# Windowed attention and token/channel mixer on one core: the first batch's units in one written list, and other groups of u with an identity matmul

## The chip, the cores and the metric

The kernel runs on one core of one Trainium2 chip. The metric is the device time of one execution in microseconds (us). The engines are called as in the profile: PE (TensorE matmuls), PEld (its weight loads), DVE (VectorE), ACT (ScalarE), POOL (GpSimd), SP (SyncE).

## The reference, cut to what matters

Four batches, 8 heads, 768 rows, head size 64. Each row attends to the 128 rows that end with itself and to the first four rows (the sinks). The heads' results side by side are x (768 x 512 for a batch), which goes through two mixers:

```python
scores = scale * np.matmul(q, k.transpose(0, 1, 3, 2))
keep = is_sink | in_window
a = np.exp(scores - max) ; a = a / np.sum(a)          # over the kept keys
x = np.matmul(a, v)                                   # heads side by side
h = np.maximum(x.T @ w_tok1, 0.0) @ w_tok2            # along the 768 rows
u = x + h.T
out = u + np.maximum(u @ w_ch1, 0.0) @ w_ch2          # along the 512 columns
```

## The kernel before, in words

Heads go in pairs, four pairs to a batch (p = 0 to 3 in the first). q and k of the first batch's pairs are loaded by SP and cast on chip by ACT, DVE or POOL (POOL for pair 3); all later ones come by casting loads that POOL issues. The work on PE is cut into **units**. A unit names its PE cost, what it depends on, how many banks of PSUM it needs, and the operations on other engines that follow it (`then`). There are two banks' worth of `sc` (scores, two physical banks each) and four `mx` banks. Units of the first batch, by the names that the change gives them (p the pair, g a group):

- **q0, k0, ...**: `turn` (L429) transposes q or k of a pair into two `mx` banks; two copies by ACT or DVE (L402, lines 129 and 131 in the profile) make qT, kT.
- **m00, m01, ...**: `masked` (L484) writes the additive mask of pair p, key group g into a score bank with identity matmuls (`ps_sc<-mask_add,ident`). All but m30 exist; s30 is masked afterwards, on DVE (L547).
- **s00, ...**: `scores` (L499) adds the scores into that bank (`ps_sc<-qT,kT`); then ACT takes the exponential (L539, `pT`). g is 0, 1, 2; g = 2 is narrower (768 columns for 1024).
- **x1, x3**: `score_sinks` (L561), the sink scores of two pairs (`ps_mx<-qT,kT`), then an exponential (L578).
- **o00, o01, ...**: `pv` (L586), probabilities times v for half the rows, in one `mx` bank; then DVE takes the reciprocal of the sums (L607) and normalises into x_sb (L610).
- **h00, h01, h10, h11**: `mix_h` (L706), x times w_tok1 for column group g (g = 0 is pairs 0 and 1) and half t of the 256 token features; a relu on ACT or DVE makes h1T.
- **u00, u02, u04, u10, u12, u14**: `mix_u` (L734), h times w_tok2 for group g and two row tiles from st. With `by_pe`, x is added in PSUM by one identity matmul for each row tile, and the result may be copied out by ACT or DVE; without, DVE alone takes it out and adds x (L751).
- **t00, ...**: `transpose_u` (L800) transposes these two row tiles of u (`ps_mx<-ident,u_sb`); a copy makes uT.

Then the channel mixing of batch 0 starts: `v1` (L892, `ps_mx<-uT,w_ch`), which needs both column groups of uT. The attention of the later batches is woven into it.

What orders the work is a planner that runs as the program is built (`Plan.run`, L319). It keeps a clock for each engine, with costs written beside each operation, and writes out, step after step, the unit or operation that can begin first by these clocks. There are three sources of PE units: `main` (channel mixing), `side` (attention and token mixing of later batches, placed behind `main` units as the list MERGED says; k4 and q4, the turned k and q of pair 4, are its first two) and `first` (the first batch). `first` holds several lists, in falling priority. At each step only the heads of the lists are looked at, and the first list whose head can begin within 40 ns of the soonest is taken (95 ns when staying in 64-row matmuls):

```python
early = [(t, u) for u in first if u for t in [self.start_pe(u[0])] if t is not None]
if early:
    soonest = min([t for t, _ in early] + ([] if t is None else [t]))
    stay = [(t, u) for t, u in early if self.half and u[0].half and t <= soonest + SWITCH]
    te, u = next((e for e in stay + early if e[0] <= soonest + (SWITCH if e in stay else 40.0)), (None, None))
```

Operations on ACT, DVE and POOL are taken whenever they can begin first, on the engine that would end them first. On the chip each engine then runs its instructions in the written order. `first_attention` (L822) gives six lists: scores, masks, turns, values (o), the token mixing of group 1, that of group 0. The order that came out on PE, read off the trace:

```
q0 k0 m00 m01 s00 s01 q1 m02 k1 s02 m10 x1 s10 m11 q2 s11 o00 m12 k2 s12 o01 m20 q3 s20 m21 k3 s21 o10 m22 o11
s22 s30 x3 h00 m31 m32 s31 s32 o20 o21 h01 o30 o31 u00 u02 u04 h10 h11 t00 t02 t04 u10 u12 u14 t10 t12 t14
```

With `by_pe` are u00, u02, u04 and u12.

Of the kernel before, what the change touches and what calls it, by code (L numbers as in the profile page):

```python
# [16 lines left out]
def kernel(  # L17
# [16 lines left out]
    NT = S // P  # L34
# [5 lines left out]
    NTOK = DTOK // P  # L40
    NHP = H // 2
# [11 lines left out]
    )  # L53
    NQ = 6
    NPT = 3
# [65 lines left out]
    def mm(*args, **kwargs):  # L121
        in_order(nc.tensor.matmul(*args, skip_group_check=True, **kwargs))  # L122
# [28 lines left out]
    def keep_warm(n, slot):  # L151
# [18 lines left out]
        out=ident, in_=ident, compare_op=ALU.not_equal, fill=1.0, base=0, pattern=[[-1, P]], channel_multiplier=1,  # L170
    ))
    in_order(nc.gpsimd.affine_select(
        out=mask_add[:, :, 0], in_=mask_add[:, :, 0], compare_op=ALU.is_ge,
# [3 lines left out]
        out=mask_add[:, :, 1], in_=mask_add[:, :, 1], compare_op=ALU.is_ge,  # L177
# [16 lines left out]
    for n in range(4):  # L194
# [3 lines left out]
            out=v_sink_f[rows, odd::2, i, 0:D],  # L198
# [167 lines left out]
    def burst(*pieces):  # L366

        need = {}
        for p in pieces:
            for tag, banks in p.need.items():  # L370
                need.setdefault(tag, []).extend(banks)

        def run():
            for p in pieces:
                p.fn()

        op = unit(
            sum(p.size for p in pieces), run, [d for p in pieces for d in p.deps], need,
            [t for p in pieces for t in p.then], half=True,
        )  # L380
        for p in pieces:
            for key in p.keys:
                done[key] = op
        return op
# [44 lines left out]
    def turn(p, n):  # L429

        name = ("q", "k")[n]

        def run():
            ps = [bank("mx", NT, D, dtype=BF16) for _ in range(2)]
            tiles["ps_" + name, p] = [t.rearrange("d j p -> d p j") for t in ps]
            for j in range(NT):
                for x in range(2):
                    rows = ds(D * x, D)
                    in_order(nc.tensor.transpose(ps[x][:, j], bfs[p, n][rows, j], ident[rows, rows]))

        readers = [[op] for op in done[name + "T", p]]
        done["t" + name, p] = unit(
            180, run, [done[name + "_bf", p]], {"mx": readers}, [op for r in readers for op in r], half=True,
        )
        return done["t" + name, p]
# [38 lines left out]
    def masked(p, g):  # L484

        def run():
            ps = tiles["ps_s", p, g] = bank("sc")
            for i in range(2):
                mm(
                    of_keys(ps)[:, i, 0:width(g)], ident,  # L490
                    mask_adds[g == 0].rearrange("p k n q -> p (k n q)")[:, 0:width(g)], start=True, stop=False,
                )

        x = done["exp", p, g] = Op({}, None)
        deps = [done["tk", 0]] if p == 0 else []
        done["mask", p, g] = unit(width(g) * 0.84, run, deps, {"sc": [[x]]})
        return done["mask", p, g]

    def scores(p, g):  # L499

        by_pe = ("mask", p, g) in done
        quarters = p >= NHP and g > 0

        def by_halves(ps):
            for k in range(2):
                kt = 2 * g + k
                nq = 2 if kt < NT - 1 else 1
                for i in range(2):  # L510
                    mm(
                        of_keys(ps)[:, i, ds(2 * k * P, nq * P)], tiles["kT", p][ds(D * i, D), ts(kt, P)],
                        tiles["qT", p][ds(D * i, D), kt * P:(kt + nq) * P], start=not by_pe, stop=True,
                    )

        def by_quarters(ps):
            for k in range(2):
                for y in range(2):
                    a = 4 * g + 2 * k + y
                    nq = min(3, 2 * NT - a)  # L520
                    for i in range(2):
                        rows = ds(D * i, D)
                        mm(
                            ps[ds(D * y, D), i, k, y:y + nq], tiles["kT", p][rows, ts(a, D)],
                            tiles["qT", p][rows, D * a:D * (a + nq)], start=True, stop=True,
                        )

        def run():
            if ("pT", p) not in tiles:
                tiles["pT", p] = pt_pool.tile([P, 2, NT, 2, P], BF16, name="pT")  # L530
            if not by_pe:
                tiles["ps_s", p, g] = bank("sc")
            (by_quarters if quarters else by_halves)(tiles["ps_s", p, g])

        def part(t):
            return t.rearrange("p i k n q -> p i (k n q)")[:, :, 0:width(g)]

        def exp(e):
            in_order(nc.scalar.activation(  # L539
                part(tiles["pT", p][:, :, ds(2 * g, 2)]), of_keys(tiles["ps_s", p, g])[:, :, 0:width(g)], AF.Exp,  # L540
                scale=scale,
            ))

        def mask(e):
            pt = part(tiles["pT", p][:, :, ds(2 * g, 2)])
            m = part(mask_first if g == 0 else mask_main)
            in_order(nc.vector.tensor_tensor(out=pt, in0=pt, in1=m, op=ALU.mult))  # L547

        x = done["exp", p, g] if by_pe else Op({}, None)
        x.cost, x.fn, x.deps = {"ACT": 190.0 + 1.5 * width(g)}, exp, [("pv", p - NPT)] if p >= NPT else []  # L550
        x.urgent = 2 * (p < NHP)
        then = [x]
        if not by_pe:
            then.append(Op({"DVE": 100.0 + 1.2 * width(g)}, mask, [x, done["masks"]]))
            then[-1].urgent = 2 * (p < NHP)
        done["p", p, g] = then[-1]
        deps = [*done["qT", p], *done["kT", p]] if g else [done["qT", p][0], done["kT", p][0]]
        deps += [done["mask", p, g]] if by_pe else []
        return piece((190, 165, 140)[g] if quarters else width(g) * 0.47, run, deps, {} if by_pe else {"sc": [[x]]}, then, [("s", p)])

    def score_sinks(p):  # L561


        def run():
            pT_sink = pt_pool.tile([P, (NT - 2) * P], BF16, name="pT_sink")
            tiles["ps_sk", p] = bank("mx", (NT - 2) * P)
            for n in (p - 1, p):
                tiles["pT_sink", n] = pT_sink
                for i in range(2):
                    rows = ds(D * i, D)  # L570
                    c = ODD * (n % 2)
                    mm(
                        tiles["ps_sk", p][ds(D * i + c, ODD)], tiles["kT", n][rows, 0:ODD],
                        tiles["qT", n][rows, 2 * P:], start=True, stop=True,
                    )

        def exp(e):
            in_order(nc.scalar.activation(tiles["pT_sink", p], tiles["ps_sk", p], AF.Exp, scale=scale))  # L578

        x = Op({"ACT": 580.0}, exp, [("pv", p - NPT)] if p >= NPT else [])  # L580
        for n in (p - 1, p):
            done["p", n, NT] = x
        deps = [d for m in (p - 1, p) for d in [done["kT", m][0], *done["qT", m]]]
        return piece(225, run, deps, {"mx": [[x]]}, [x], [("sk", p - 1), ("sk", p)])
# [236 lines left out]

    def first_attention():  # L822

        for p in range(NHP):
            prepare(p)
        turned = [turn(p, n) for p in range(NHP) for n in range(2)]
        masks, scored, out = [], [], []
        for p in range(NHP):
            for g in range(NT // 2):
                if (p, g) in MASKED_BY_PE:  # L830
                    masks.append(masked(p, g))
                scored.append(burst(scores(p, g)))
                if g == 0 and p == NHP - 1:
                    scored.append(burst(score_sinks(p)))
            if p == 1:
                out.append(burst(score_sinks(p)))
            if p % 2:
                out += [pv(n, half) for n in (p - 1, p) for half in range(2)]
        tokens = []
        for g in range(2):  # L840
            tokens.append([mix_h(0, g, t, 1) for t in range(NTOK)])
            tokens[g] += [mix_u(0, g, st, 2, g == 0 or st == 2) for st in range(0, NT, 2)]
            tokens[g] += [transpose_u(0, g, st, 2) for st in range(0, NT, 2)]
        return scored, masks, turned, out, *tokens[::-1]

    def attention_and_tokens():

# [247 lines left out]
```

## Time and profile before

| what | value |
|---|---|
| median of 3 runs | 207.12 us (206.72 to 207.36) |
| the profiled execution's own time | 206.41 us |
| its span, first to last instruction | 204.6 us |
| granted TensorE clock over the span | 1.000 |
| PE matmuls, busy | 197.6 us |
| the landing of w_tok1 (issued by POOL at 11.39) | 18.9 us |
| first matmul of v1 (channel mixing of batch 0) | 30.46 us |

All other times in the text are of the profiled execution, counted from the start of its span. A row of the timeline is a run of like instructions on one engine: start, length, engine, line, operation, output<-inputs, shape, count, and in brackets how long the engine was idle before it and what released it. Matmuls are pipelined: a row's length has the way through the array in it, so how long a unit holds PE is read from the starts of matmuls, from one unit to the next. `mm` (L121) and `transpose` (L124) record most of PE's work, so units are told apart by their tiles.

### The profile page before, as it was taken

To read this page: it belongs to the slowest core of one execution; us is meant where nothing else is said; L and a number is where in the kernel's file an instruction comes from. 1 tells how busy PE (TensorE), PEld (TensorE's weight loads), DVE (VectorE), ACT (ScalarE), POOL (GpSimd) and SP (SyncE) were. 2 spreads that over 40 slices of the span, in tenths; PEclk is the share of its full clock that TensorE was granted. 3 is DMA by queue.
4 is the path that set the end of the run, shared out by engine and by line. 5 is a ranking of instruction groups with operands and counts; after the bars stand their busy time and mean duration, and the time that the engine had idled before them with its cause. 6 is when DMAs were issued, how large, how long until landed. Compare 5 with 4: busy or idle time off the path is not lost.

```text
span 204.6 us, 5496 instructions
## 1 busy us (share of the span) xinstructions
PE 197.6 (97%) x2377; PEld 119.3 (58%) x2377; DVE 112.4 (55%) x238; ACT 113.8 (56%) x195; POOL 67.3 (33%) x86
## 2 busy tenths in 40 slices
PE   6798999999999999999999999999999999999994
PEld 2345985566665665667656545666655645665453
DVE  4775653657788766866948557572654361001222
ACT  4898668879706535886563145886750114773000
POOL 6299859795699891450000000000000000000000
DMA  6999999999999999193001112100002112000223
GB/s 193 292 257 188 169 177 191 160 172 206 157 180 189 187 184 198 22 128 20 3 0 54 53 64 97 51 5 0 0 3 103 51 54 103 0 3 0 103 103 103
DMA packets 73223, 21.58 MB, mean 105 GB/s; under 512 B 63216, under 2 KB 70256, under 8 KB 73200
## 3 DMA queue, kind: packets, MB, share of 16 engines
q0 software_dynamic: 67232, 11.80, 73.1%
q1 hardware_dynamic: 5968, 9.45, 13.1%
q8 instruction: 18, 0.29, 0.6%
q14 instruction: 5, 0.04, 0.1%
HBM read 26.75 MB, written 6.29 MB: 161 GB/s over the span
## 4 chain that ended last, share of the span: by engine, by line
PE 85%; DMA 6%; DVE 3%; ACT 2%; POOL 1%; issue 1%; SPq 0%; POOLq 0%; ACTq 0%
PE ps_mx L122 77%; PE ps_sc L122 4%; DMA w_tok<-in_moe_w_tok_dram 4%; DMA v_sink_f<-in_v_dram 2%; PE ps_sc L455 2%; POOL v_aug L115 1%; DVE kT L131 1%; PE ps_mx L427 1%; ACT pT L539 1%; ACT qT L129 1%; PE ps_mx L125 1%; SPq L197 0%; ACT uT L129 0%; DVE u_sb L751 0%; DVE x_sb L650 0%
## 5 line engine op out<-in xcount | busy, mean ns | idle before, releaser
L122 PE MATMUL ps_mx<-uT,w_ch 128*128 128x384 bf16 x384 | 67.1, 326 | 0.1
L122 PE MATMUL ps_mx<-w_ch,v1T 128*128 128x512 bf16 (+2 forms) x312 | 66.9, 363 | 0.0
L539 ACT ACTIVATE pT<-ps_sc 128x1024 bf16<-128x1024 f32 (+1 forms) x48 | 44.4, 952 | 13.0 <-PE ps_sc L122 12.9
L122 PEld LDWEIGHTS <-w_ch 128*128 128x128 bf16 x384 | 36.0, 98 | 23.9 <-issue 1.2
L135 ACT ACTIVATE v1T<-ps_mx 128x384 bf16<-128x384 f32 x77 | 37.7, 490 | 19.5 <-PE ps_mx L122 18.9
L122 PEld LDWEIGHTS <-v1T 128*128 128x128 bf16 x312 | 28.3, 98 | 27.6 <-issue 0.5
L924 DVE TENSOR_TENSOR o_sb<-ps_mx,u_sb 128x512 f32<-128x512 f32 x23 | 15.8, 687 | 34.6 <-PE ps_mx L122 34.6
L122 PEld LDWEIGHTS <-w_tok 128*128 128x128 bf16 x192 | 18.3, 98 | 5.9 <-DMA w_tok<-in_moe_w_tok_dram 0.7
L107 POOL DMA_DIRECT2D q_bf<-in_q_dram x24 | 19.6, 822 | 4.4 <-DMA w_ch<-in_moe_w_ch_dram 2.2
L107 POOL DMA_DIRECT2D k_bf<-in_k_dram x24 | 19.6, 820 | 4.1 <-DMA w_ch<-in_moe_w_ch_dram 1.7
L751 DVE TENSOR_TENSOR u_sb<-ps_mx,x_sb 128x512 bf16<-128x512 f32 x20 | 13.2, 687 | 13.0 <-PE ps_mx L122 12.9
L115 POOL DMA_DIRECT2D v_aug<-in_v_dram x16 | 16.4, 1026 | 8.3 <-ACT v_sink L129 7.1
L131 DVE COPY kT<-ps_sc 128x768 bf16<-128x768 bf16 x11 | 10.5, 958 | 13.4 <-ACT qT L129 13.4
L122 PEld LDWEIGHTS <-pT 128*128 128x128 bf16 x352 | 14.1, 98 | 3.3 <-issue 0.6
L129 ACT ACTIVATE qT<-ps_sc 128x768 bf16<-128x768 bf16 x11 | 8.9, 810 | 12.3 <-PE ps_sc L455 12.1
L122 PE MATMUL ps_mx<-v_aug,pT 128*128 128x65 bf16 x352 | 15.6, 194 | 0.0
L547 DVE TENSOR_TENSOR pT<-pT,mask_main 128x1024 bf16<-128x1024 bf16 (+1 forms) x24 | 14.3, 619 | 1.3 <-ACT pT L539 1.3
L122 PE MATMUL ps_sc<-qT,kT 64*64 64x192 bf16 (+3 forms) x288 | 14.4, 248 | 0.0
L135 ACT ACTIVATE h1T<-ps_mx 128x512 bf16<-128x512 f32 (+1 forms) x8 | 4.1, 517 | 17.1 <-PE ps_mx L122 16.9
L122 PE MATMUL ps_mx<-h1T,w_tok 128*128 128x256 bf16 x96 | 13.2, 273 | 0.0
L137 DVE TENSOR_SCALAR v1T<-ps_mx 128x384 bf16<-128x384 f32 x19 | 10.4, 549 | 4.9 <-PE ps_mx L122 4.9
L122 PE MATMUL ps_mx<-x_sb,w_tok 128*128 128x256 bf16 x96 | 12.0, 273 | 0.5 <-DMA w_tok<-in_moe_w_tok_dram 0.4
(68 smaller groups left out, 156.6 us busy)
## 6 DMA issues: line engine op xcount, KB each, us to landing
out_dram<-o_sb SPq DMA_DIRECT2D x23, 256.0 KB, 2.0
v_aug<-in_v_dram POOLq DMA_DIRECT2D x16, 192.0 KB, 7.2
w_ch<-in_moe_w_ch_dram POOLq DMA_DIRECT2D x8, 384.0 KB, 8.8
q_bf<-in_q_dram POOLq DMA_DIRECT2D x24, 96.0 KB, 6.8
k_bf<-in_k_dram POOLq DMA_DIRECT2D x24, 96.0 KB, 5.9
q_f<-in_q_dram SPq DMA_DIRECT2D x4, 384.0 KB, 5.0
k_f<-in_k_dram SPq DMA_DIRECT2D x4, 384.0 KB, 5.7
w_tok<-in_moe_w_tok_dram POOLq DMA_DIRECT2D x2, 384.0 KB, 7.7
```

Source lines behind the costliest of these rows:

```text
L107: in_order(nc.gpsimd.dma_start(out=out[:, h], in_=rows[:, h]))
L115: in_order(nc.gpsimd.dma_start(out=v_aug.rearrange("p i t d -> p (i t) d")[:, :, 0:D], in_=v[b].rearrange("h s d -> (h s) d")[2 * hp * S:2 ...
L122: in_order(nc.tensor.matmul(*args, skip_group_check=True, **kwargs))
L129: in_order(nc.scalar.activation(out, in_, AF.Copy))
L131: in_order({"DVE": nc.vector, "POOL": nc.gpsimd}[e].tensor_copy(out=out, in_=in_))
L135: in_order(nc.scalar.activation(out, in_, AF.Relu))
L137: in_order(nc.vector.tensor_scalar_max(out=out, in0=in_, scalar1=0.0))
L455: in_order(nc.tensor.transpose(ps[:, x, n, j], bfs[p, n][rows, j], ident[rows, rows]))
L539: in_order(nc.scalar.activation(part(tiles["pT", p][:, :, ds(2 * g, 2)]), of_keys(tiles["ps_s", p, g])[:, :, 0:width(g)], AF.Exp, scale=scale,
L547: in_order(nc.vector.tensor_tensor(out=pt, in0=pt, in1=m, op=ALU.mult))
L751: in_order(nc.vector.tensor_tensor(out=u_part(b, g, s0, n), in0=tiles["ps_u", b, g, s0], in1=x_sb[b][:, s0:s0 + n, c0:c0 + cn], op=ALU.add,))
L924: in_order(nc.vector.tensor_tensor(out=o_sb.rearrange("p (g c) -> p g c", g=2), in1=u_rows(b, st), in0=tiles["ps_out", b, st].rearrange("p ...
```

## The change

`first_attention` makes the same units, but gives them a name each and returns one list, in the order of the new constant FIRST_BATCH. So the planner sees one head at a time: the order of these units on PE is the written one. Which engine makes a copy, the place of the operations of ACT and DVE, and the choice of PSUM banks still come from the planner's clocks. `main` and `side` may still go before a head that would begin over 40 ns later.

Against the order of before: s01 before s00; k1 before m02; o01 before m12 k2 s12; s20 before q3; m22 o11 s22 o10 s30 for o10 m22 o11 s22 s30; m31 h01 m32 and h00 after o21, for h00 m31 m32 and h01 after o21; u02 before u00. And x is added by identity matmuls in u02, u12 and u14, where it was u00, u02, u04 and u12.

```diff
+    FIRST_BATCH = (
+        "q0 k0 m00 m01 s01 s00 q1 k1 m02 s02 m10 x1 s10 m11 q2 s11 o00 o01 m12 k2 s12 m20 s20 q3 m21 k3 s21 "
+        "m22 o11 s22 o10 s30 x3 m31 h01 m32 s31 s32 o20 o21 h00 o30 o31 u02 u00 u04 h10 h11 t00 t02 t04 u10 "
+        "u12 u14 t10 t12 t14"
+    )
...
         for p in range(NHP):
             prepare(p)
-        turned = [turn(p, n) for p in range(NHP) for n in range(2)]
-        masks, scored, out = [], [], []
+        made = {}
+        for p in range(NHP):
+            for n in range(2):
+                made["qk"[n] + str(p)] = turn(p, n)
         for p in range(NHP):
             for g in range(NT // 2):
                 if (p, g) in MASKED_BY_PE:
-                    masks.append(masked(p, g))
-                scored.append(burst(scores(p, g)))
-                if g == 0 and p == NHP - 1:
-                    scored.append(burst(score_sinks(p)))
-            if p == 1:
-                out.append(burst(score_sinks(p)))
+                    made[f"m{p}{g}"] = masked(p, g)
+                made[f"s{p}{g}"] = burst(scores(p, g))
             if p % 2:
-                out += [pv(n, half) for n in (p - 1, p) for half in range(2)]
-        tokens = []
+                made[f"x{p}"] = burst(score_sinks(p))
+                for n in (p - 1, p):
+                    for half in range(2):
+                        made[f"o{n}{half}"] = pv(n, half)
         for g in range(2):
-            tokens.append([mix_h(0, g, t, 1) for t in range(NTOK)])
-            tokens[g] += [mix_u(0, g, st, 2, g == 0 or st == 2) for st in range(0, NT, 2)]
-            tokens[g] += [transpose_u(0, g, st, 2) for st in range(0, NT, 2)]
-        return scored, masks, turned, out, *tokens[::-1]
+            for t in range(NTOK):
+                made[f"h{g}{t}"] = mix_h(0, g, t, 1)
+            for st in range(0, NT, 2):
+                made[f"u{g}{st}"] = mix_u(0, g, st, 2, (g, st) in [(0, 2), (1, 2), (1, 4)])
+            for st in range(0, NT, 2):
+                made[f"t{g}{st}"] = transpose_u(0, g, st, 2)
+        return [[made[name] for name in FIRST_BATCH.split()]]
```

## The prediction, made before the changed kernel was run

> **What bounds the kernel now.** I read the page first, then the chain that ended last in order of time, then the timelines of PE, ACT and DVE up to 31 us. The page:
>
> ```profile
> span 204.6 us, 5496 instructions
> PE 197.6 (97%) x2377; PEld 119.3 (58%) x2377; DVE 112.4 (55%) x238; ACT 113.8 (56%) x195; POOL 67.3 (33%) x86
> PE 85%; DMA 6%; DVE 3%; ACT 2%; POOL 1%; issue 1%; SPq 0%; POOLq 0%; ACTq 0%
> ```
>
> PE is busy for 97% of the span, so the end moves by the PE work that goes and by the PE pauses that close. The change touches the first batch alone, and the chain shows where that batch hands over:
>
> ```profile
> 11.39 7.51 DMA w_tok<-in_moe_w_tok_dram
> 18.95 0.83 PE ps_mx L122 x6
> ...
> 27.53 1.54 PE ps_mx L122 x14
> 29.08 0.02 issue
> 29.10 0.70 DVE u_sb L751
> 29.80 0.05 issue
> 29.85 0.40 PE ps_mx L125 x4
> 30.25 0.28 PE ps_mx L439 x12
> 30.53 1.41 PE ps_mx L122 x8
> ```
>
> Up to 18.95 us w_tok1's landing leads; then PE; then a wait for an addition on DVE (u14) before t14; then k4 and the first v1 of the channel mixing (start 30.46 on PE). From there to 201.7 us matmul starts in the trace lie more than 0.2 us further apart than their widths only at 70.56, 72.73 and 98.75, so a shift of the 30.46 goes through to the end. PE before that:
>
> ```profile
> 15.78 0.35 PE L439 MATMUL ps_mx<-ident,k_bf 64*128 64x64 bf16 x12 [0.36 <-POOL k_bf L131]
> 17.62 0.56 PE L122 MATMUL ps_sc<-qT,kT 64*128 64x256 bf16 x8
> 18.95 0.83 PE L122 MATMUL ps_mx<-x_sb,w_tok 128*128 128x256 bf16 x6 [0.45 <-DMA w_tok<-in_moe_w_tok_dram]
> 20.47 0.56 PE L122 MATMUL ps_sc<-qT,kT 64*128 64x256 bf16 x8
> 23.43 0.27 PE L122 MATMUL ps_mx<-x_sb,ident 128*128 128x256 bf16 x1
> ```
>
> and ACT with its exponentials (the second row is s22 and s30, the third s31 and s32):
>
> ```profile
> 16.59 1.02 ACT L539 ACTIVATE pT<-ps_sc 128x1024 bf16<-128x1024 f32 x1
> 18.00 1.73 ACT L539 ACTIVATE pT<-ps_sc 128x768 bf16<-128x768 f32 x2 [0.40 <-PE ps_sc L122]
> 20.90 1.73 ACT L539 ACTIVATE pT<-ps_sc 128x1024 bf16<-128x1024 f32 x2 [0.69 <-PE ps_sc L122]
> ```
>
> To be seen: ACT waits 0.40 us for s22 and 0.69 us for s31, because PE sends o10, m22 and o11 ahead of s22, then stops 0.45 us at h00 for the weights with m31 and m32 queued behind it. The order on PE makes these pauses.
>
> **Prices**, from starts on PE: turn 0.18 us; m 0.43 (narrow g=2: 0.32); s 0.23 (0.15); x 0.21; o 0.38 (first half), 0.55 (second); h 0.65; t 0.22; one identity matmul of u 0.109, so a u is 0.65 with and 0.44 without. Exponentials follow each other on ACT every 0.90 us (0.76 for 768 columns). From a matmul's last column to its reader on ACT or DVE 0.21 us (u12's last matmul starts at 28.35, its reader at 28.66); from an ACT or DVE end to PE 0.05.
>
> **The switch.** Last matmul of m32 starts at 20.210 and streams 0.162, s31 starts at 20.469: 0.10 us for going from 128-row to 64-row matmuls. The list has two more such changes (s22, o10, s30 for s22, s30); they are in the walk below. The Trainium skill, TensorEngine Tiling (Array Packing), section Key Properties, says that a change of tiling mode drains TensorE, which speaks against the new order. The trace agrees, with 0.10 us each; counted fully the two would be 0.2 us of the forecast, and without them it would be 206.3.
>
> **Early part (to 15.78).** s01 goes ahead of s00. s01 needs the second half of kT0 (ACT, to 7.08), s00 only the first, so ACT's first exponential starts at 7.57 (7.13 + 0.12 + 0.11 + 0.21) for 7.33: 0.24 us late. ACT is dense from there to 14.47, so this is carried. k1 ahead of m02 comes 0.3 us earlier (its cast ends at 8.46), o01 ahead of k2 makes kT2 later: k2 at about 13.5 for 12.71, s12's exponential at 14.0 to 14.25 for 13.71. Against this, s20 no longer stands behind q3 (which waits for POOL's cast at 14.26), so its exponential can start by about 15.0 for 15.17. All meets at k3: POOL ends its cast at 15.72, and POOL's order holds no PE result, so k3 stays at 15.78. m22 needs s20's exponential over by 16.24; it is over at 15.9 to 16.05. I take the early part at 0; ends: -0.1 and +0.5.
>
> **Middle part, by start on PE.** s21 15.97; m22 16.30; o11 16.62; s22 17.27, its exponential 17.63 (18.00 before; ACT is done with s21's at 17.49); o10 17.52; s30 18.00; x3 18.33; m31, whose bank s22's exponential leaves at 18.49, 18.64 (19.62 before); h01 19.07, weights there since 18.9; m32, bank free at 19.51, 19.73; s31 20.15, its exponential 20.59 (20.90 before); s32 20.38; o20 20.63 instead of 20.96. **-0.33 us.** The same five units as before follow (2.47 us), so the first u starts at 23.10. Ends: 0 (h01 or m32 wait as long as h00 did) and -0.45 (the whole stop).
>
> **Late part.** Group 0's u lose two pairs of identity matmuls: 4 x 0.109 = -0.44. Group 1 gains one pair: +0.22. **Net -0.22.** u00, u04 and u10 are now added on DVE (0.69 each, where an ACT copy is 0.60). u00 would be read at 24.4 to 25.1 and u04 to 25.8, behind the normalisations of o30 and o31; their transposes come at 25.9 and 26.4, so this is hidden by h10 and h11 (1.31 us); without that cover it would cost up to 0.7. h10 needs o31 normalised by 24.63, and that is over at about 24.3. u10 at 26.61, u12 27.05, u14 27.70, t10 28.35. u10's addition, on DVE after two uT copies as before, is over by 28.0. u12's copy ends on ACT at 28.51: t12 at 28.57 without the 0.19 of before. u14 can now go to ACT: 28.56 to 29.16, t14 29.22, an idle 0.43 in place of 0.30. **-0.08.** What is late next is this copy, on which t14, k4 and v1 stand. Ends: 0.69 on DVE behind two copies, +0.5; or k4 in the idle 0.43, -0.28.
>
> No unit here issues a DMA, and SP's and POOL's queues keep their order. Loads follow each other by landings: k of pair 5 lands at about 24.73 + 7.6 = 32.3, its use is at 33.7, so 0.6 us earlier still fits.
>
> **Sum.** -0.33 - 0.22 - 0.08 = -0.63: v1 starts at 29.83. The profiled execution took 206.41 (its span 204.6 and 1.8 around it), below the runs' 206.72 to 207.36; it would become 205.8. The median 207.12 becomes **206.5**.
>
> **Rivals.**
> 1. *ACT's early delay is not absorbed.* If ACT also takes both halves of kT2 and of kT1 (0.38 each), s20's exponential ends past 16.24 and m22, s22 and all behind them slip by 0.3 to 0.5: 206.8 to 207.0. For it: ACT is dense from 7.3 to 14.5. Against: DVE has pauses there.
> 2. *It does not do what it says.* The order is worked out in the planner's costs, and its landing and copy times are not the chip's: the heads of the one list wait where three lists had another unit. If h01 or m32 pauses as h00 did (-0.33 gone) and t14 waits on DVE (+0.3): 207.1 to 207.2. Against: the walk uses measured rows and finds no pause over 0.1 us between 16 and 28.5.
> 3. *More.* k4 falls into t14's wait, or the stops at 70.56 and 72.73 (0.2 each) close: 205.9 to 206.2. Against: k4 wants two of four banks, which are full of t and u then.
> 4. *Slower, at 70.56.* The planner shares the copies between ACT and DVE by its own clock, which the change shifts. There the chain runs over ACT (pT, uT, qT) and DVE (kT 0.96, reciprocals, x_sb 0.56) and PE already waits 0.2. One more relu (0.55) or uT copy (0.96) put ahead on DVE is a wait of its full length; from 0.63 on the gain is gone, and with both of them, or the same at 98.75, +0.9: 207.4 to 208.0. For it: a full DVE from 68.4 to 70.5. Against: the order of PE from 30.18 on is fixed and its needs are unchanged.
>
> **Numbers.** A difference of 0.3% (0.62 us) is about what a measurement of this kernel can tell from none; the forecast stands on that bound. Forecast (206.2 to 206.8) 0.52, rival 1 0.14, rival 2 0.08, rival 3 0.12, rival 4 0.14. Faster by over 0.3%: rival 3 and somewhat over half of the forecast case, 0.44. Slower by over 0.3%: the greater part of rival 4, 0.12. Within: 0.44. For 8 in 10 the range leaves out the far parts of rivals 3 and 4: 205.9 to 207.5.
>
> **What would show it.** Early: first exponential near 7.6, k3 at 15.78. Middle: s22's exponential near 17.6, m31 before h01 with no long wait, o20 near 20.6. Late: six identity matmuls of x_sb for eight, t12 without a wait, v1 at 29.8. Wrong if k3 or s21 starts later than 16.0, if o20 is not before 20.9, if t00 or t04 waits for DVE, or if PE pauses over 0.3 us stand at 66 to 73 or near 98.

## The result, and the profile after

The changed kernel takes 206.17 us (median of 8 runs, 205.60 to 206.46), the kernel before beside it 206.98 (8 runs, 206.50 to 207.81): ratio 0.9955, interval 0.9937 to 0.9973, about 0.9 us less. Two further comparisons, among the experiments, gave 0.9983 (0.9962 to 1.0003) and 0.9972 (0.9948 to 0.9996). The mean of the three is 0.9970, or 0.62 us of 207. The forecast was 206.5 us, 0.63 us less.

The profiled execution of the changed kernel took 206.46 us, as long as the longest of its 8 runs; that of before, 206.41, was shorter than any of its own. So laid side by side these two show no gain, and the first task is to see why. The page of the changed kernel:

```profile
span 204.7 us, 5470 instructions
PE 197.8 (97%) x2355; PEld 120.0 (59%) x2375; DVE 113.9 (56%) x241; ACT 112.5 (55%) x192; POOL 67.3 (33%) x86
PE 88%; DMA 3%; ACT 3%; DVE 3%; issue 1%; SPq 1%; ACTq 0%
```

The third line is the share of each engine in the chain that ended last: DMA has fallen from 6% to 3%. The chain itself, in order of time (start, length, what), in two stretches:

```profile
2.24 6.41 DMA k_f<-in_k_dram
...
8.67 0.57 DVE k_bf L136
...
15.16 0.71 ACT pT L544
15.87 0.04 issue
15.91 0.59 PE ps_sc L127 x2
16.50 0.28 PE ps_mx L444 x12
...
19.73 0.82 PE ps_mx L127 x6
...
```

```profile
29.23 0.61 ACT u_sb L134
29.83 0.05 issue
29.88 0.40 PE ps_mx L130 x4
...
```

Two things are new. The row at 19.73 is h01, and it now stands behind PE's own work; before, the row at that place, h00, stood behind w_tok1's landing. And the copy ahead of t14 is ACT's (u14, line 134), where it was an addition on DVE. The v1 that closes the batch starts at 30.49 on PE, for 30.46 before: the loads arrived later in this execution. DVE's first cast of q ended at 8.22 instead of 7.48, POOL's chain of work began with the landing of v_sink at 9.61 instead of 8.83, and POOL's cast for k3 ended at 16.34 instead of 15.73. PE from there, on the timeline:

```profile
16.43 0.35 PE L444 MATMUL ps_mx<-ident,k_bf 64*128 64x64 bf16 x12
17.90 0.34 PE L127 MATMUL ps_sc<-qT,kT 64*128 64x256 bf16 x4
18.64 0.39 PE L127 MATMUL ps_sc<-qT,kT 64*128 64x256 bf16 x4
19.29 0.39 PE L127 MATMUL ps_sc<-mask_add,ident 128*128 128x512 bf16 x1
19.73 0.82 PE L127 MATMUL ps_mx<-x_sb,w_tok 128*128 128x256 bf16 x6
23.77 0.27 PE L127 MATMUL ps_mx<-x_sb,ident 128*128 128x256 bf16 x1
29.88 0.40 PE L130 MATMUL ps_mx<-ident,u_sb 128*128 128x128 bf16 x4 [0.24 <-ACT u_sb L134]
```

These are k3, s22, s30, m31, h01, the first u and t14. From k3 to h01 no bracket shows a pause; the one for the weights (0.45 us before) is gone. ACT's exponentials:

```profile
17.20 2.96 ACT L544 ACTIVATE pT<-ps_sc 128x1024 bf16<-128x1024 f32 x3
21.25 1.73 ACT L544 ACTIVATE pT<-ps_sc 128x1024 bf16<-128x1024 f32 x2 [0.27 <-PE ps_sc L127]
```

s21, s22 and s30 follow each other without the 0.40 us of before, and s31 waits 0.27 where it waited 0.69. The start differs between executions, whatever the kernel, so the stages are compared by lengths from k3's start on, all from starts on PE (us, good to 0.01):

| profiled execution | k3 starts | k3 to o20 | o20 to first u | to h10 | to t10 | to t14 | to v1 | k3 to v1 | v1 to last matmul |
|---|---|---|---|---|---|---|---|---|---|
| before | 15.78 | 5.18 | 2.47 | 1.96 | 3.51 | 0.95 | 0.61 | 14.68 | 171.00 |
| before, again | 15.87 | 5.59 | 2.47 | 1.97 | 3.51 | 0.94 | 0.62 | 15.10 | 170.99 |
| changed | 16.43 | 4.87 | 2.47 | 1.53 | 3.73 | 0.85 | 0.61 | 14.06 | 171.00 |
| changed, again | 15.95 | 4.87 | 2.48 | 1.52 | 3.73 | 0.85 | 0.61 | 14.06 | 171.00 |
| changed, third | 16.84 | 4.87 | 2.48 | 1.52 | 3.73 | 0.85 | 0.61 | 14.06 | 171.00 |

From k3 on the changed kernel repeats to 0.01 us; the kernel before does not, and all of its scatter is in one column, k3 to o20. What v1 starts then takes 171.00 us in both.

### The profile page after: what moved, and what is told of

Same layout as the page of the kernel before. It is cut to its first block, busy times and chain, and to the rows that moved or that the text cites. A ratio compares the mean times of both kernels' runs of the same rounds, so it can differ in the third digit from the quotient of the medians.

```text
span 204.7 us, 5470 instructions
## 1 busy us (share of the span) xinstructions
PE 197.8 (97%) x2355; PEld 120.0 (59%) x2375; DVE 113.9 (56%) x241; ACT 112.5 (55%) x192; POOL 67.3 (33%) x86
## 4 chain that ended last, share of the span: by engine, by line
PE 88%; DMA 3%; ACT 3%; DVE 3%; issue 1%; SPq 1%; ACTq 0%
PE ps_mx L127 77%; PE ps_sc L127 6%; DMA k_f<-in_k_dram 3%; PE ps_sc L460 2%; ACT pT L544 1%; PE ps_mx L444 1%; DVE kT L136 1%; PE ps_mx L432 1%; ACT qT L134 1%; SPq L99 1%; DVE x_sb L655 1%; PE ps_mx L130 1%; ACT uT L134 0%; DVE o_sb L933 0%; ACT u_sb L134 0%
## 5 line engine op out<-in xcount | busy, mean ns | idle before, releaser
L127 PE MATMUL ps_mx<-w_ch,v1T 128*128 128x512 bf16 (+2 forms) x295 | 65.1, 362 | 1.1 <-issue 0.3
L933 DVE TENSOR_TENSOR o_sb<-ps_mx,u_sb 128x512 f32<-128x512 f32 x23 | 15.8, 688 | 34.6 <-PE ps_mx L127 34.6
L756 DVE TENSOR_TENSOR u_sb<-ps_mx,x_sb 128x512 bf16<-128x512 f32 x21 | 13.8, 687 | 12.8 <-PE ps_mx L127 12.5
L127 PE MATMUL ps_sc<-qT,kT 64*64 64x192 bf16 (+3 forms) x288 | 15.0, 252 | 0.1
L127 PEld LDWEIGHTS <-kT 64*64 64x64 bf16 (+2 forms) x320 | 7.7, 101 | 8.0 <-issue 4.7
```

Source lines behind the costliest of these rows:

```text
L756: in_order(nc.vector.tensor_tensor(out=u_part(b, g, s0, n), in0=tiles["ps_u", b, g, s0], in1=x_sb[b][:, s0:s0 + n, c0:c0 + cn], op=ALU.add,))
L933: in_order(nc.vector.tensor_tensor(out=o_sb.rearrange("p (g c) -> p g c", g=2), in1=u_rows(b, st), in0=tiles["ps_out", b, st].rearrange("p ...
```

## The experiments

Open after the result were: what in the old order makes k3 to o20 long and variable (the pauses of ACT, as the prediction had it, or w_tok1's landing alone); whether the identity matmuls pay by themselves; and what the early part is worth, since k3 itself starts anywhere from 15.8 to 17.1. The rival theories were that the order of s22 and s31 in front of ACT does it, and that the new early order makes POOL's chain to k3 shorter. The three groups below ran on one chip each, every kernel against the kernel before on the same chip.

**The two parts of the change, apart**

*The changed kernel and the kernel before, again.*

> The changed kernel once more, unaltered, for a second profile and time. Theory A (the gain lies behind k3: the order of the middle part 0.33 us, one pair of identity matmuls less 0.22, the wait before t14 0.08): 0.3 to 0.6% below the kernel before; from the start of k3 to the first v1 14.05 us where the first profile of before has 14.68; if loads land as early as in the profile of before, k3 at 15.8 and v1 at 29.8. Theory B (the early order gives 0.2 to 0.3 as well): k3 or its s21 earlier than in before by that much for the same landing of k.

> The kernel before once more, for a second profile. Theory A: k3 to v1 14.68 again when w_tok1 lands as late after k3 as in the first profile (3.1 us); the landing times and the time at which PE leaves half clock may differ by some 0.7 us from one execution to the next, as the two first profiles did (first q cast on DVE at 6.92 and 7.66).

Measured: ratio 0.9983 (0.9962 to 1.0003) for the changed kernel. The second profile of the kernel before, on PE:

```profile
15.87 0.35 PE L439 MATMUL ps_mx<-ident,k_bf 64*128 64x64 bf16 x12
...
19.45 0.83 PE L122 MATMUL ps_mx<-x_sb,w_tok 128*128 128x256 bf16 x6 [0.77 <-DMA w_tok<-in_moe_w_tok_dram]
```

w_tok1 took 8.0 us from its issue for 7.5, so h00 stopped PE for 0.77 us instead of 0.45, and o20 came at k3 + 5.59. In the changed kernel it landed at 18.7, and h01, which stands 3.30 us behind k3, took it at 19.26 without a stop.

*The order alone*: the old set of identity matmuls.

```diff
-                made[f"u{g}{st}"] = mix_u(0, g, st, 2, (g, st) in [(0, 2), (1, 2), (1, 4)])
+                made[f"u{g}{st}"] = mix_u(0, g, st, 2, g == 0 or st == 2)
```

> The new list, with the identity matmuls as before (u00, u02, u04, u12). Theory A: half of the gain stays, ratio about 0.9985; k3 to o20 4.85 us as in the changed kernel (5.18 in before), then u02 to t10 longer by 0.22 and t14 waiting for DVE by 0.4 to 0.5: k3 to v1 about 14.35. Rival (the identity matmuls alone carry the gain): ratio 1.000, k3 to v1 14.68.

Measured: ratio 1.0000 (0.9975 to 1.0025). k3 to v1 is 14.38: o20 to u, u to h10 and the rest are those of before, 0.32 above the changed kernel, as the identity term says (0.44 - 0.22 + 0.10). But v1 to the last matmul is 171.34, and so the whole gain is lost. PE and DVE of this kernel, where 0.19 of the 0.34 stands:

```profile
45.55 1.65 PE L127 MATMUL ps_mx<-uT,w_ch 128*128 128x384 bf16 x8
```

```profile
44.54 0.96 DVE L136 COPY kT<-ps_sc 128x768 bf16<-128x768 bf16 x1 [2.40 <-ACT qT L134]
...
45.80 0.53 DVE L142 TENSOR_SCALAR v1T<-ps_mx 128x384 bf16<-128x384 f32 x1
```

The same eight matmuls take 1.46 us in the changed kernel. Here a gap lies in them, up to 46.39, just after DVE's relu of v1 at 45.80 to 46.33 has given its bank back. Counted from v1, that relu and the copy of kT ahead of it are 0.44 us later than in the changed kernel. 0.15 us of that came down from an earlier gap, at 34.16 (below). The rest began on ACT, with the copy of qT that the copy of kT waits for; this kernel, then the changed one:

```profile
43.70 0.81 ACT L134 ACTIVATE qT<-ps_sc 128x768 bf16<-128x768 bf16 x1 [0.33 <-ACT v1T L140]
```

```profile
43.00 0.81 ACT L134 ACTIVATE qT<-ps_sc 128x768 bf16<-128x768 bf16 x1
```

ACT stood idle for 0.33 us although its own relu and the transposes that it copies were over by 43.37. It is not another order: behind v1 the two traces have the same operations, tiles and shapes in the same order on PE, DVE and ACT. Ahead of v1 this kernel has two more instructions on ACT, and that makes the copy the 64th that the trace holds of ACT. In two more kernels, the next one and the early part alone, the copy is also the 64th; it waits 0.33 us there, and v1 to the last matmul takes 171.17 and 171.18. In the other eleven profiles it is the 62nd or the 65th to 67th and waits 0.03. Why the 64th waits, no view shows. The other 0.15 of the 0.34 is the gap at 34.16, in the turn of k5: the second half of k5's load landed at 34.12 in this execution, 9.1 us after its issue, where it took 8.1 in the changed kernel; none of the other thirteen profiles has this gap. So neither part of the 0.34 is rival 4, copies shared out in another way.

*The identity matmuls alone*: the old order, written as the list, with the new set.

```diff
-        "q0 k0 m00 m01 s01 s00 q1 k1 m02 s02 m10 x1 s10 m11 q2 s11 o00 o01 m12 k2 s12 m20 s20 q3 m21 k3 s21 "
-        "m22 o11 s22 o10 s30 x3 m31 h01 m32 s31 s32 o20 o21 h00 o30 o31 u02 u00 u04 h10 h11 t00 t02 t04 u10 "
+        "q0 k0 m00 m01 s00 s01 q1 m02 k1 s02 m10 x1 s10 m11 q2 s11 o00 m12 k2 s12 o01 m20 q3 s20 m21 k3 s21 o10 m22 o11 "
+        "s22 s30 x3 h00 m31 m32 s31 s32 o20 o21 h01 o30 o31 u00 u02 u04 h10 h11 t00 t02 t04 u10 "
```

> The order of before, written as one list, with the identity matmuls of the change (u02, u12, u14). Theory A: 0.30 us of the gain, ratio about 0.9985; k3 to v1 about 14.38, h00 still stopped by the weights. Rival (only the order matters): ratio 1.000 and 14.68.

Measured: ratio 1.0016 (0.9995 to 1.0038). PE, and ACT and DVE in the stretch after:

```profile
20.27 0.83 PE L127 MATMUL ps_mx<-x_sb,w_tok 128*128 128x256 bf16 x6 [1.54 <-DMA w_tok<-in_moe_w_tok_dram]
...
26.37 0.65 PE L444 MATMUL ps_mx<-ident,k_bf 64*128 64x64 bf16 x12
26.95 1.48 PE L127 MATMUL ps_mx<-x_sb,w_tok 128*128 128x256 bf16 x12
```

```profile
26.04 0.60 ACT L134 ACTIVATE u_sb<-ps_mx 128x512 bf16<-128x512 f32 x1 [1.61 <-PE ps_mx L127]
```

```profile
25.39 0.69 DVE L756 TENSOR_TENSOR u_sb<-ps_mx,x_sb 128x512 bf16<-128x512 f32 x1
26.00 0.55 DVE L615 TENSOR_TENSOR x_sb<-ps_mx,recip 128x384 bf16<-128x384 f32 x1
```

w_tok1 took 8.9 us here, the stop is 1.54, and o20 stands at k3 + 6.46. The identity matmuls gain nothing either: first u to v1 is 7.03 us, as before, against 6.72 in the changed kernel. With u00 first, DVE took its addition (25.39) ahead of the normalisation of o31 (to 26.55), which h10 reads; in the changed kernel that normalisation came first. k4 went into the hole ahead of h10, and in its middle waited 0.29 us for a bank that ACT's copy of u02 (26.04 to 26.64) gave back. That u02 first would by itself keep DVE free and let ACT copy early is read from these rows; it was not tried alone.

**The landing and the start**

*Weights early*, in the old kernel (old order, old set) and in the changed one: w_tok1 is queued on POOL by an earlier pair. Only that is edited in the second.

```diff
-        if p == NHP - 2:
+        if p == 1:
```

> The kernel before with w_tok1's load issued one place earlier on POOL (behind v of pair 1 instead of pair 2, about 1.0 us earlier). Theory W (the stop of PE at h00 until the weights land is what the new order covers): h00 starts at k3 + 2.65 without a DMA wait, k3 to o20 falls from 5.18 and 5.59 in the two profiles of before to about 4.9, v1 to about k3 + 14.4, and the time to about that of the changed kernel plus 0.3: ratio 0.997 to 0.999. Rival E (ACT's waits for s22 and s31 are set by the order itself): k3 to o20 stays at 5.18, ratio 0.999 to 1.000.

> The changed kernel with the same earlier issue of w_tok1's load. Theory W: nothing changes, k3 to o20 4.87 and k3 to v1 14.06, because h01 already comes after the landing; ratio to the kernel before as for the changed kernel (0.995 to 0.998). Rival: a shorter time, if the weights still hold h01 in executions in which they land late (7.1 to 8.9 us from issue were seen).

Measured: the old order 1.0009 (0.9988 to 1.0030), the new one 0.9972 (0.9949 to 0.9996). The old order, on PE:

```profile
16.85 0.35 PE L444 MATMUL ps_mx<-ident,k_bf 64*128 64x64 bf16 x12 [0.37 <-POOL k_bf L136]
...
19.50 0.83 PE L127 MATMUL ps_mx<-x_sb,w_tok 128*128 128x256 bf16 x6
...
24.78 0.39 PE L127 MATMUL ps_mx<-h1T,w_tok 128*128 128x256 bf16 x2 [0.29 <-DMA w_tok<-in_moe_w_tok_dram]
```

With the weights there, h00 starts at k3 + 2.65 without a stop, and o20 at k3 + 4.90: within 0.03 us of the new order's 4.87, although o10 m22 o11 still stand ahead of s22. So the landing sets the difference between the two orders. ACT's pause is not nothing: with the weights there, m32 waits 0.24 us for ACT, up to k3 + 3.99. But the new order, which reaches m32 at k3 + 3.96, has spent 0.20 us on its two further changes between 64-row and 128-row matmuls (s22, o10 and s30 hold PE for 1.07 us, for 0.87 in the old order), and the two nearly cancel. The wait came back at the next load: w_tok2 is read by u00 (the row at 24.78), landed 9.5 us after its issue, and cost 0.46 in all. In the changed kernel nothing moves with the weights early (k3 to o20 4.87), as the landing theory says.

*The early part undone*: the list's first line back to the old order.

```diff
-        "q0 k0 m00 m01 s01 s00 q1 k1 m02 s02 m10 x1 s10 m11 q2 s11 o00 o01 m12 k2 s12 m20 s20 q3 m21 k3 s21 "
+        "q0 k0 m00 m01 s00 s01 q1 m02 k1 s02 m10 x1 s10 m11 q2 s11 o00 m12 k2 s12 o01 m20 q3 s20 m21 k3 s21 "
```

> The changed kernel with the early part of its list put back (s00 s01; m02 before k1; m12 k2 s12 before o01; q3 before s20). Theory A2 (the early order costs: in the second profile of the changed kernel k3 began 0.37 us after its cast had ended): k3 begins 0.05 to 0.12 us after the end of its cast, k3 to v1 stays 14.06, and the time is at or up to 0.15% below the changed kernel: ratio 0.995 to 0.998. Rival B (the early order gives): ratio nearer to 1.000, k3 to v1 longer by 0.2 or more, because s20's exponential ends later and m22 waits.

Measured: ratio 1.0007 (0.9985 to 1.0028). From k3 on it is the changed kernel (14.06); but k3 itself started at 17.11, the loads being late (v_sink's cast starts at 9.91). One such run does not tell the order from the loads; hence a second one below.

*k's last cast on DVE instead of POOL*, on the kernel with the early part undone: if POOL's chain holds k3, this frees it.

```diff
-        cost = {"POOL": 850.0} if p == NHP - 1 else {"DVE": 570.0} if p or n else {"ACT": 850.0}
+        cost = {"POOL": 850.0} if p == NHP - 1 and n == 0 else {"DVE": 570.0} if p or n else {"ACT": 850.0}
```

> early_undone with k of pair 3 cast by DVE (0.56 us) and not by POOL (0.84, behind the issue of w_tok2's load). Theory A2 (the changed kernel's first batch hangs on k3): k3 starts 0.3 to 0.6 us earlier, v1 follows by 0.2 to 0.5 until the landing of w_tok1 plus 10.8 holds it; ratio 0.993 to 0.996. Rival: DVE waits for k's landing with the normalisation of o01 and q3's copy behind it, and v1 comes no earlier: ratio as for early_undone.

Measured: ratio 0.9992 (0.9969 to 1.0016); the expectation failed. DVE, then PE:

```profile
15.30 0.52 DVE L136 CAST k_bf<-k_f 128x768 bf16<-128x768 f32 x1
```

```profile
16.02 0.61 PE L127 MATMUL ps_sc<-mask_add,ident 128*128 128x512 bf16 x2
16.56 0.36 PE L444 MATMUL ps_mx<-ident,k_bf 64*128 64x64 bf16 x12
...
17.44 0.48 PE L127 MATMUL ps_sc<-mask_add,ident 128*128 128x384 bf16 x2 [0.31 <-ACT pT L544]
```

The cast ended at 15.82, no earlier than POOL's, because DVE had other work ahead of it; then k3 stood 0.74 us behind its own cast, held by m21 in front of it, and m22 waited for ACT. Several chains arrive at k3 within half a microsecond.

**The start once more, and k4 in the last wait**

*The changed kernel a third time, and the early part undone a second time.*

> The changed kernel a third time, as the measure for the other three on the same chip. Theory P (the early order also shortens POOL's chain from the v_sink cast to k3's cast: 6.70 to 6.79 us without load waits in the four profiles with the new early order, 6.79 to 7.23 in the five with the old one, because casts on DVE and load issues on POOL then hold each other up less): 6.7 again; k3 within 0.4 us of the cast's end, k3 to v1 14.06; ratio to the kernel before 0.995 to 0.999.

> early_undone a second time, on the same chip as the changed kernel. Theory P: POOL's chain 6.9 to 7.2 us, k3 0.05 to 0.1 after the cast's end, k3 to v1 14.06; 0.1 to 0.4% above the changed kernel. Rival A2 (the early order costs by holding k3 behind m21): at or below the changed kernel, POOL's chain the same in both.

Measured: 0.9972 (0.9948 to 0.9996) and 0.9970 (0.9948 to 0.9993): no difference. Each early order has its own loss. The changed kernel's third profile, and the undone one's second, both on PE:

```profile
16.32 0.59 PE L127 MATMUL ps_sc<-mask_add,ident 128*128 128x512 bf16 x2
16.84 0.35 PE L444 MATMUL ps_mx<-ident,k_bf 64*128 64x64 bf16 x12
```

```profile
15.81 0.35 PE L444 MATMUL ps_mx<-ident,k_bf 64*128 64x64 bf16 x12
15.99 0.38 PE L127 MATMUL ps_sc<-qT,kT 64*128 64x256 bf16 x4
16.53 0.48 PE L127 MATMUL ps_sc<-mask_add,ident 128*128 128x384 bf16 x2 [0.15 <-ACT pT L544]
```

In the first, k3's cast had ended at 16.17, and k3 stood 0.67 us behind it because m21, ahead of k3, came late. In the second, k3 follows its cast by 0.06, but m22 waits for s20's exponential, and o20 comes at k3 + 5.07. Over all profiles k3 stands 0.06 to 0.67 us behind its cast with the new early order (0.09, 0.37 and 0.67 in the changed kernel), and 0.05 to 0.12 with the old one, k3_by_dve aside. The time from the start of v_sink's cast to the end of k3's cast, less what POOL waits for a load (0.61 and 0.31 us in the changed kernel's second and third profile, 0.21 in the old order with the new identity set), is 6.71 to 7.06 us with the new and 6.77 to 7.23 with the old, weights queued early left out: the theory that the new early order shortens POOL's chain falls.

*The early part alone*: the rest of the list and the identity set as before.

```diff
-        "m22 o11 s22 o10 s30 x3 m31 h01 m32 s31 s32 o20 o21 h00 o30 o31 u02 u00 u04 h10 h11 t00 t02 t04 u10 "
+        "o10 m22 o11 s22 s30 x3 h00 m31 m32 s31 s32 o20 o21 h01 o30 o31 u00 u02 u04 h10 h11 t00 t02 t04 u10 "
...
-                made[f"u{g}{st}"] = mix_u(0, g, st, 2, (g, st) in [(0, 2), (1, 2), (1, 4)])
+                made[f"u{g}{st}"] = mix_u(0, g, st, 2, g == 0 or st == 2)
```

> Only the early part of the new list; its middle and late part and the identity matmuls as before. Theory W with P: h00 stops for w_tok1 again, v1 comes 11.5 us after h00, so the shorter POOL chain helps only through w_tok1's earlier issue: ratio 0.998 to 1.001. Rival (the early order carries the gain): 0.995 to 0.998.

Measured: ratio 0.9999 (0.9976 to 1.0022). PE:

```profile
18.98 0.83 PE L127 MATMUL ps_mx<-x_sb,w_tok 128*128 128x256 bf16 x6
...
20.21 0.48 PE L127 MATMUL ps_sc<-mask_add,ident 128*128 128x384 bf16 x2 [0.18 <-ACT pT L544]
```

h00 started at k3 + 2.76, only 0.11 us late, w_tok1 having landed at 18.94 with k3 at 16.22. Then m32 waited for ACT up to k3 + 3.99, and o20 came at k3 + 4.90: again the old middle order costs 0.03 us when the weights are there. 0.19 of the loss is a wait behind v1, at 46.12, by the late 64th instruction of ACT.

*k4 and q4 in t14's wait.* The prediction's third rival had k4 fall into the wait ahead of t14, and put against it that the banks were full. Here the turns of pair 4 write one bank of `ps_sc` each and stand in the list ahead of t14; the two places that the static order gave them are taken out.

```diff
-        "1/0 0/2 2/4 3/8 4/15 5/17 6/17 7/19 8/24 9/25 10/25 11/27 12/27 13/29 14/29 15/30 16/32 17/32 18/35 "
+        "2/4 3/8 4/15 5/17 6/17 7/19 8/24 9/25 10/25 11/27 12/27 13/29 14/29 15/30 16/32 17/32 18/35 "
...
-        "u12 u14 t10 t12 t14"
+        "u12 u14 t10 t12 kq4 t14"
...
-        parts = 2 if p <= NHP else 1
+        parts = 2 if p < NHP else 1
...
+        prepare(NHP)
+        made["kq4"] = burst(transposed(NHP))
...
-        prepare(first)
-        units += [turn(first, n) for n in range(2)]
+        units += [None, None]
```

> A version of my own: the changed kernel with q and k of pair 4 turned by one unit into a score bank (as the later pairs are) and this unit put into t14's wait for the copy of u14. t12 to t14 0.78 us in place of 0.63, v1 right behind t14, so k3 to v1 13.8 in place of 14.06; q4 with its two mode changes gone from the stretch behind v1, so v1 to the last matmul 170.6 in place of 171.0: 0.2 to 0.3% below the changed kernel. Rival: scores of pair 4 wait for the bank to be cleared and for the whole copies of q and k (0.8 to 0.96 us), and v1 to the last matmul stays at 171.0 or grows.

Measured: 205.96 us (median of 10 runs) against 207.11, ratio 0.9944 (0.9922 to 0.9966); the changed kernel on the same chip had 206.33, 0.9972. It is the fastest of the kernels tried, though its interval and that of the changed kernel overlap. PE:

```profile
28.84 0.61 PE L130 MATMUL ps_mx<-ident,u_sb 128*128 128x128 bf16 x8
29.38 0.35 PE L460 MATMUL ps_sc<-ident,q_bf 64*128 64x64 bf16 x12
29.57 0.34 PE L460 MATMUL ps_sc<-ident,k_bf 64*128 64x64 bf16 x12
29.84 0.40 PE L130 MATMUL ps_mx<-ident,u_sb 128*128 128x128 bf16 x4
30.07 2.92 PE L127 MATMUL ps_mx<-uT,w_ch 128*128 128x384 bf16 x16
```

t10 and t12, both turns, t14, v1: t14 has no bracket, the wait for u14's copy is filled, and v1 starts 13.82 us after k3 for 14.06. Behind v1 170.74 us are left for 171.00, because q4 is done too.

## Why the prediction held, step by step

**Middle part: the size held, the reason only in part.** The walk from k3 was exact: m31, h01, s31, o20 (k3 + 4.87, forecast 4.85), the first u (7.34, forecast 7.32) and v1 (14.06, forecast 14.05) stand where it put them. But "the order on PE makes these pauses" was the smaller part of the cause. In the old order h00 waits for w_tok1, and in every profile with it o20 is the later of k3 + 4.90 and the landing + 2.05 (the row of h00 to o20 takes 2.01). With the weights early the old order loses 0.03 us and not 0.33, though s22 stands where it stood: the 0.24 us that PE then waits for ACT is about what the new order pays for its two further switches, which the walk had right with 0.10 each. What the new order gains is cover: h01 is read 3.30 us after k3 where h00 was at 2.65, with m31 ahead of it. Worked out from that, the gain for one and the same landing can lie between 0.03 (landing early) and about 0.45 (landing + 2.05 against landing + 0.04 and the 1.56 from h01 to o20); in no profile did h01 wait, so the upper end is not shown. w_tok1's landing, 6.6 to 8.9 us after its issue, decides. The forecast's ends, 0 and -0.45, have nearly these sizes but not these conditions: it put 0 where h01 waits for the weights, and there the gain would be largest.

**Late part: right in each term.** Group 0 forecast -0.44, measured -0.43 (u to h10, 1.96 to 1.53); group 1 forecast +0.22, measured +0.22 (h10 to t10); t14's wait forecast -0.08, measured -0.10, and u14 went to ACT as said. The run without the new identity set gave the same sum, 14.38 for 14.06. What the prediction had not seen is that this needs the order: it took u00's addition to stand behind the normalisations of o30 and o31, as it did in the changed kernel, but in the old order DVE took it ahead of o31's, k4 went ahead of h10, and the same edit brings nothing.

**Early part: 0 was neither shown nor refuted.** The prediction called itself wrong if k3 started later than 16.0 or o20 came after 20.9. Both happened in the first profile (16.43 and 21.30). Of k3's 0.65 us, 0.61 came with POOL's cast, by later loads, and 0.04 with m21. Those marks should have been lengths from k3, not times from the span's start. One term of this part did not come: the first exponential, forecast 0.24 us late because of s01 ahead of s00. It starts 1.74 us after the end of k0's cast both before (5.58 to 7.33) and in the changed kernel's second profile (5.91 to 7.66); s01 stood behind the masks and did not wait for the second half of kT0. Rival 1 is there in part: m21, behind ACT's exponential, held k3 by up to 0.67 us in one execution. The old early order has a loss of its own (m22, up to 0.20 in k3 to o20). With 0.9955, 0.9983 and 0.9972 for the whole change, and 1.0007 and 0.9970 with the early part undone, no effect of it can be told from none; a difference of 0.2% would be missed.

**The other rivals.** The planner's landing times did not betray the list (rival 2): no stop over 0.1 us stands from k3 to u10. The stop at 70.56 kept its length: v1 to the last matmul takes 171.00 in both, so rival 4 did not come true, nor in the run of the order alone, where the order behind v1 is that of the changed kernel. What cost 0.34 us there were two things that the prediction had not on its list: a late start of one instruction on ACT, and a late landing of k5, for which "0.6 us earlier still fits" had counted on the landing of one execution. Rival 3 needed another bank, and then paid (kq4).

**The sum.** -0.63 was forecast, -0.9 measured first and about -0.62 as a mean of three. The spread is as wide as the comparison's intervals and as the landing's part (0.03 to 0.45). That the mean agrees to 0.01 is chance. Open is why the loads' landing varies between executions, and why the 64th instruction of ACT starts late.

## What to carry to other kernels

When the start of a kernel varies by a microsecond between executions, compare stages by their lengths from an event inside the kernel, and write the marks of a prediction that way too. A stop at a load's first reader is worth what the load happens to be late: putting ready work ahead of that reader buys cover, and the gain is a spread, not a number. A cheaper edit can pay only together with an order that fits it; try the parts apart before counting them as a sum. And when a part alone loses elsewhere, compare the two traces instruction by instruction before blaming the order.

## What the runs showed of the hardware

PE's first matmuls ran at half speed in some executions. The first four masks of the changed kernel's third profile, and of the kernel with the early part undone:

```profile
6.06 1.89 PE L127 MATMUL ps_sc<-mask_add,ident 128*128 128x512 bf16 x4
```

```profile
5.75 1.04 PE L127 MATMUL ps_sc<-mask_add,ident 128*128 128x512 bf16 x4
```

They start 0.43 us apart in the first and 0.22 in the second, for the same instructions, while the granted clock is given as 1.00 over this stretch in both. In eight of the fourteen profiles some of the four masks ran so, in six of them all four; the last slow matmuls stand between about 6 and 11 us, and no stage behind k3 shows it. The first exponential starts 1.74 to 1.81 us after the end of k0's cast where all masks ran fast, and 2.56 to 2.97 where all four ran slow. The Trainium skill, TensorE: Matmul & The Clock Gate, section "Wait — 56ns, not 53.3ns?", gives 426.7 and 215.7 ns between the starts of matmuls of 512 columns with the array cold and warm, and the trace agrees. The Trainium skill says on the same page, section "What's actually happening", that the number of cold matmuls varies from run to run; the fourteen profiles agree.

DVE's casts and POOL's DMA issues lengthen each other. The issue of w_tok1 on POOL, before and with the early part undone:

```profile
11.39 1.03 POOL L140 DMA_DIRECT2D w_tok<-in_moe_w_tok_dram  x1
```

```profile
12.91 0.83 POOL L145 DMA_DIRECT2D w_tok<-in_moe_w_tok_dram  x1
```

A cast on DVE (11.45 to 12.01) lay inside the first, which took 1.03 us; the last cast had ended at 12.29 ahead of the second: 0.83. The loss can fall on the other side: the cast of q at 9.68 in the kernel before, beside an issue of v, took 1.08 us instead of 0.55. The Trainium skill, SBUF — State Buffer, section "SBUF: two separate sides", says that DVE, in operations that use two ports, locks the port which the issuing of such a DMA needs; the trace agrees in kind, with 0.2 to 0.5 us for each meeting. That the casts here are such operations, no run shows.
